# A tile of their own for the score maxima, the row sums finished on VectorE, spread reciprocals a slot later, and early weights converted one step a period

## Chip, cores and metric

The kernel runs on one core of a Trainium2 chip. The metric is the device time of one execution in microseconds (us).

## What is computed

Causal attention over 2 batches, 12 heads, 448 positions and 64 features a head, and then two gated layers over the 896 tokens:

```python
scores = scale * np.matmul(q, k.transpose(0, 1, 3, 2))
scores = np.where(mask, -1000000000.0, scores)
scores = scores - np.max(scores, axis=-1, keepdims=True)
attn = np.exp(scores)
attn = attn / (np.sum(attn, axis=-1, keepdims=True) + 1e-09)
x = np.matmul(attn, v)                            # regrouped to 896 x 768
x = (1/(1+exp(-(x @ w_gate))) * (x @ w_val)) @ moe_w_out
h = x @ w_in                                      # 896 x 1024
solu = h * softmax(h); ln = normalised solu * g_ln
out = ln @ moe2_w_out                             # 896 x 768
```

## The kernel before

All five engines run instruction streams in an order that is written out by hand (`manual_schedule`). Each engine takes its own stream in order, so an instruction that waits holds up everything behind it on its engine. Waits between engines follow from which tiles, and which parts of them, instructions read and write. Matrix products are made exact enough by splitting each operand into a rounded hi part and a lo remainder and multiplying three pairs of parts.

**The attention stage** handles 12 head pairs (`NPR`), one every 8 slots (`PER`, a period). The table `STEPS` gives each step a slot relative to the start of its pair, an engine and a function; the loop over slots `s` emits for each slot the TensorE steps first ('E'), then ScalarE ('A'), VectorE ('D') and GpSimd ('P'). A pair's steps reach over some 23 slots, so three pairs overlap. For one pair p, with the slots before the change:

- keys and queries: casts on GpSimd (`prep_k_hi`, slot -7, and `prep_q_hi`, -6) and remainders on VectorE (`prep_k_lo`, -5, line 229, and `prep_q_lo`, -2, line 249). `prep_q_lo(p)` also issues the load of pair p+2 on SP's queue. Pair 0 is prepared ahead of the loop.
- scores: `sc_mm` at slots 0 and 4 puts the causal mask into PSUM with bf16 matmuls (line 329) and adds the score matmuls (line 338). Query tiles 3 and 0 (448 and 64 keys) share one PSUM tile, tiles 2 and 1 (320 and 192 keys) another.
- `sc_max` on VectorE (slots 0, 1, 4, 5; line 351, for the very first tile line 349) writes negated row maxima; `sc_exp` on ScalarE (slots 1, 2, 5, 6; line 358) makes the exponentials and the row sums. Maxima and sums of a pair lie in one tile of 16 columns, `sum_t`: sums in columns 0 to 7, maxima in 8 to 15, those of one query tile four columns apart (`8 + i:16:NQ`).
- `sums` on GpSimd (slot 7, line 363) adds an epsilon to the sums, `recips` on VectorE (slot 8, line 367) takes reciprocals, `rs_wide` on GpSimd spreads them over columns (slot 8, line 221), `rs_mm` on TensorE transposes them (slot 10, line 381) and `rs_out` on ScalarE copies the result out of PSUM (slot 11).
- the exponentials are transposed on TensorE (`tr_mm`, slots 9, 11, 13, 15; line 409), cast on ScalarE a slot later (`tr_hi`, line 416) and their remainder taken on VectorE two slots later (`tr_lo`, line 229); two PSUM tiles take turns. The products with the values are eight chunks on TensorE (`pv_mm`, slots 13 to 20; line 441).
- the values are split on GpSimd (`prep_v_hi`, slot 7, and `prep_v_lo`, 9); `last_keys` is a small GpSimd copy (3). `x_mul` on VectorE multiplies by the reciprocals (21), `x_hi` on ScalarE casts (22) and `x_lo` on GpSimd takes the remainder (23).

`keep_warm(n)` issues n small matmuls whose result nobody reads (line 308): 56 ahead of the loop and 24 each at slots 2, 5 and 9.

**Weights** arrive as 64-bit floats, 768 KB a chunk, and are converted in four steps (`bits_steps`): a scaling on ScalarE (line 112), then a shift (115) and two combinations (117, 120) on VectorE; after the last step the next chunk's load is issued on SP's queue. `chunk_hi` (ScalarE, 131) and `chunk_lo` (VectorE, 134) split a chunk. In the attention stage the loop converts chunks 0 to 3, one every nine slots from slot 88 on, and splits chunks 0 and 1.

**The early tile.** From slot 96 on (`PER * NPR`) the loop emits up to two matmuls a slot of the next stage's first tile (`early_tiles`, line 473; 36 in all, 18 with each of chunks 0 and 1), as far as their chunk has been split. What is left follows the loop. The next stage then starts at line 574; its `start_chunk(c)` splits chunk c+1 and converts chunk c+2 if nobody has.

Of the kernel before, what the change touches and what calls it, by code (L numbers as in the profile page):

```python
# [44 lines left out]
def attn_moe_moe2(ctx: ExitStack, tc: tile.TileContext, qk, v, w_gv, w_out, w_in2, w_out2, g_ln, out):  # L45
# [16 lines left out]
    maskb = const.tile([128, 128], BF16, name="maskb")  # L62
# [127 lines left out]
    with ExitStack() as actx:  # L190
# [94 lines left out]
        nc.vector.tensor_copy(out=maskb, in_=mask0)  # L285
# [6 lines left out]
        sum_t = [one.tile([128, 16], F32, name=f"sum{i}") for i in range(3)]  # L292
# [26 lines left out]
        def sc_mm(p, g):  # L319
            both = ps_s.tile([128, 2, 512], F32, tag="s", name="s")  # L320
            t = qk_sp[p]
            flat = t.rearrange("p c s -> p (c s)")
            c0 = 0
            for i in GROUPS[g]:
                n = QE[i]
                w = min(n, 128)
                ps = ps_sc[p, i] = both[:, :, c0:c0 + n]
                for e in range(2):
                    nc.tensor.matmul(out=ps[:, e, n - w:], lhsT=identb, rhs=maskb[:, 128 - w:],
                                     start=(c0 == 0), stop=False, skip_group_check=True)  # L330
                c0 += n
            for i in GROUPS[g]:
                n = QE[i]
                for m, (cq, ck) in enumerate(((1, 0), (1, 3), (2, 0))):

                    for e in range(2):
                        rows = slice(e * D, (e + 1) * D)
                        nc.tensor.matmul(out=ps_sc[p, i][:, 1 - e], lhsT=flat[rows, cq * S + n - 128:cq * S + n],  # L338
                                         rhs=t[rows, ck, :n], start=False, stop=(m == 2), skip_group_check=True)

        def sums_of(p, i, e):
            k = NQ * (1 - e) + i
            return sum_t[p % 3][:, k:k + 1], sum_t[p % 3][:, 8 + k:9 + k]

        def sc_max(p, i):
            ps = ps_sc[p, i]
            if p == 0 and i == GROUPS[0][0]:
                for e in range(2):
                    nc.vector.reduce_max(out=sums_of(p, i, e)[1], in_=ps[:, 1 - e], axis=AX.X, negate=True)
            else:  # L350
                nc.vector.reduce_max(out=sum_t[p % 3][:, 8 + i:16:NQ], in_=ps, axis=AX.X, negate=True)  # L351
# [9 lines left out]
        def sums(p):  # L361
            rs = rs_t[p] = st.tile([128, 16], F32, tag="rs", name="rs")
            nc.gpsimd.tensor_scalar(out=rs[:, 8:16], in0=sum_t[p % 3][:, 0:8], scalar1=EPS_SUM, scalar2=0.0,
                                    op0=ALU.add, op1=ALU.add)

        def recips(p):
            nc.vector.reciprocal(out=rs_t[p][:, 0:8], in_=rs_t[p][:, 8:16])
# [93 lines left out]
        def early_tiles():  # L461
# [30 lines left out]
            (10, 'E', rs_mm),  # L492
            (-7, ENG['kh'], prep_k_hi), (-6, ENG['qh'], prep_q_hi), (-5, ENG['kl'], prep_k_lo), (-2, 'D', prep_q_lo),
            (3, ENG['lk'], last_keys), (7, ENG['vh'], prep_v_hi), (9, ENG['vl'], prep_v_lo),
            (7, 'P', sums), (8, 'D', recips), (8, ENG['rx'], rs_wide), (11, ENG['rr'], rs_out),
# [6 lines left out]

        def steps(s, eng):
            for s0, e, f in STEPS:
                p, r = divmod(s - s0, PER)
                if e == eng and r == 0 and (1 if s0 < 0 else 0) <= p < NPR:
                    f(p)


        for s in range(PER * NPR + 26):  # L510
            if s in (2, 5, 9):
                keep_warm(24)
# [4 lines left out]
            steps(s, 'A')  # L517
            steps(s, 'D')
            steps(s, 'P')
            if s in (8, 12):  # L520
                dma_next()

            for c in range(2 * NE + 2):
                e = s - 88 - 9 * c
                if e == 0:
                    bits_now = bits_steps(c)
                if e in (0, 2, 4, 6):
                    next(bits_now)
                if e == 7 and c < 2 * NE:
                    chunk_hi(c)  # L530
                if e == 8 and c < 2 * NE:
                    chunk_lo(c)
# [230 lines left out]
```

## Time and profile before

| what | us |
|---|---|
| median of 3 runs | 514.14 |
| lowest and highest of them | 513.76, 514.71 |
| the profiled execution, its own time | 514.3 |
| its span, first to last instruction | 512.5 |
| TensorE busy (98% of the span) | 501.2 |
| VectorE busy (66%) | 335.9 |
| ScalarE busy (44%) | 226.4 |
| GpSimd busy (23%) | 118.0 |

In the profile PE is TensorE, PEld its weight loads, DVE VectorE, ACT ScalarE, POOL GpSimd and SP the engine that issues the DMAs. L351 is line 351 of the kernel. A row of the timeline gives start, duration, engine, line, operation, output tile and input tiles, shapes and count; square brackets hold the idle time of the engine before it and what ended that. Times are from the start of the span. Busy time of TensorE is partly modelled, and an average over stages with different limits.

### The profile page before, as it was taken

What the parts mean: (1) busy time and instruction counts of PE and PEld (TensorE: products, weight loads), DVE (VectorE), ACT (ScalarE), POOL (GpSimd) and SP (SyncE); (2) the same over time, 40 slices, a digit from 0 to 9 for tenths busy, and PEclk for the clock granted to TensorE, in tenths of its full rate; (3) what the DMA queues carried; (4) which work ended last, traced back from release to release, by engine and by line L of the source; (5) the groups of instructions that cost most, each with busy time, mean ns of one, the idle gap of its engine ahead of it and who ended that gap; (6) DMA issues with size and microseconds to landing.
All of it is one profiled execution on the core that took longest, in us unless ns stands there. A gap on an engine that the chain in (4) does not pass through costs nothing.

```text
span 512.5 us, 7699 instructions
## 1 busy us (share of the span) xinstructions
PE 501.2 (98%) x2980; PEld 457.1 (89%) x2980; DVE 335.9 (66%) x512; ACT 226.4 (44%) x481; POOL 118.0 (23%) x203
## 2 busy tenths in 40 slices
PE   8899999989999999999999999999999999999997
PEld 8888888878899999999999999999998888899997
DVE  4578787887655777887777766766753887841210
ACT  4677777784532454345434432343324242432211
POOL 3375757552000000000000000000050587710000
PEclk9899999999999999999999999999999999999999
DMA  5632323112333154355433532354440221000101
GB/s 150 184 92 77 92 79 93 42 49 76 125 123 99 66 165 164 125 163 161 137 116 125 182 123 68 139 165 164 133 176 1 86 100 62 0 32 33 61 32 61
DMA packets 13204, 52.79 MB, mean 103 GB/s; under 512 B 1776, under 2 KB 2288, under 8 KB 13168
## 3 DMA queue, kind: packets, MB, share of 16 engines
q1 hardware_dynamic: 13168, 52.31, 31.4%
q8 instruction: 23, 0.38, 0.3%
q14 instruction: 13, 0.11, 0.1%
HBM read 49.55 MB, written 2.75 MB: 102 GB/s over the span
## 4 chain that ended last, share of the span: by engine, by line
PE 81%; DVE 6%; ACT 6%; POOL 5%; issue 1%; POOLq 0%; ACTq 0%
PE gv L574 33%; PE pm L604 17%; PE po L695 12%; PE h L634 11%; ACT p L358 4%; DVE sum L351 4%; POOL v L229 2%; DVE qks L229 2%; PE gv L473 1%; PE warm L308 1%; POOL rx L221 1%; PE tp L677 1%; PE x L441 1%; PE s L338 1%; PE t L409 1%
## 5 line engine op out<-in xcount | busy, mean ns | idle before, releaser
L574 PE MATMUL gv<-xy,hl 128*128 128x448 f32 x828 | 168.1, 365 | 0.6 <-ACT pre L478 0.6
L574 PEld LDWEIGHTS gv<-xy,hl 128*128 128x128 f32 x828 | 155.5, 188 | 13.2 <-ACT pre L478 1.0
L604 PE MATMUL pm<-g,hl 128*128 128x448 f32 x432 | 87.7, 365 | 0.0
L604 PEld LDWEIGHTS pm<-g,hl 128*128 128x128 f32 x432 | 81.2, 188 | 6.4
L621 POOL TENSOR_SCALAR t<-t,g_sb 128x768 f32<-128x768 f32 x8 | 9.0, 1123 | 248.1 <-PE pm L604 248.1
L134 DVE TENSOR_TENSOR hl<-t,hl 128x768 fp32r<-128x768 f32 x36 | 35.1, 975 | 40.2 <-ACT hl L131 38.4
L695 PE MATMUL po<-wo,lt 128*128 128x384 f32 x336 | 60.7, 340 | 0.0
L634 PE MATMUL h<-wi,xy 128*128 128x512 f32 x252 | 59.2, 395 | 0.0
L695 PEld LDWEIGHTS po<-wo,lt 128*128 128x128 f32 x336 | 58.7, 188 | 0.2 <-POOL wo L626 0.2
L358 ACT ACTIVATE p<-s,sum 128x448 f32<-128x448 f32 (+3 forms) x96 | 45.0, 478 | 29.9 <-DVE sum L351 14.9
L634 PEld LDWEIGHTS h<-wi,xy 128*128 128x128 f32 x252 | 47.2, 188 | 11.4
L120 DVE SCALAR_TENSOR_TENSOR t<-raw,t 128x768 int32<-128x768 int32 (+1 forms) x56 | 53.0, 946 | 1.7
L117 DVE SCALAR_TENSOR_TENSOR t<-raw,t 128x768 int32<-128x768 int32 (+1 forms) x56 | 52.6, 939 | 1.8
L441 PE MATMUL x<-pt,v 128*128 128x320 f32 (+3 forms) x252 | 53.5, 327 | 0.0
L112 ACT ACTIVATE raw<-raw 128x768 f32<-128x768 f32 (+1 forms) x56 | 47.9, 866 | 10.3 <-DMA raw<-in_wo_dram 6.0
L351 DVE TENSOR_REDUCE sum<-s 128x2 f32<-128x128 f32 (+3 forms) x47 | 31.6, 672 | 15.2 <-ACT p L358 13.4
L441 PEld LDWEIGHTS x<-pt,v 128*128 128x128 f32 x252 | 38.1, 190 | 2.0
L229 DVE TENSOR_TENSOR pt<-t,pt 128x512 fp32r<-128x512 f32 (+1 forms) x48 | 31.9, 667 | 3.8 <-ACT pt L416 3.8
L115 DVE TENSOR_SCALAR t<-raw 128x768 int32<-128x768 int32 (+1 forms) x56 | 30.6, 547 | 4.9 <-ACT raw L112 4.9
L171 DVE TENSOR_TENSOR lt<-tp,lt 128x512 fp32r<-128x512 f32 x14 | 9.7, 690 | 36.4 <-ACT lt L170 36.4
L131 ACT CAST hl<-t 128x768 fp32r<-128x768 f32 x36 | 30.0, 832 | 4.6 <-PE pm L604 4.2
L179 ACT ACTIVATE wk<-gv 128x448 f32<-128x448 f32 x23 | 11.3, 542 | 43.1 <-PE gv L574 43.1
(90 smaller groups left out, 542.7 us busy)
## 6 DMA issues: line engine op xcount, KB each, us to landing
raw<-in_gv_dram SPq DMA_DIRECT2D x24, 768.0 KB, 4.4
raw<-in_wo_dram SPq DMA_DIRECT2D x20, 768.0 KB, 4.3
raw<-in_wi_dram SPq DMA_DIRECT2D x12, 512.0 KB, 3.5
qkr<-in_qk_dram SPq DMA_DIRECT2D x22, 224.0 KB, 3.5
vr<-in_v_dram SPq DMA_DIRECT2D x12, 256.0 KB, 2.6
out_dram<-o SPq DMA_DIRECT2D x6, 384.0 KB, 2.3
qkr<-in_qk_dram SPq DMA_DIRECT2D x4, 112.0 KB, 2.7
out_dram<-o SPq DMA_DIRECT2D x2, 192.0 KB, 1.8
```

The source lines that it names most:

```text
L112: nc.scalar.activation(out=w1.bitcast(F32), in_=w1.bitcast(F32), func=AF.Copy, scale=2.0 ** -112)
L117: nc.vector.scalar_tensor_tensor(out=tt, in0=w1, scalar=-2 ** 31, in1=tt, op0=ALU.bitwise_and, op1=ALU.bitwise_or)
L120: nc.vector.scalar_tensor_tensor(out=tt, in0=w0, scalar=29, in1=tt, op0=ALU.logical_shift_right, op1=ALU.bitwise_or)
L134: nc.vector.tensor_tensor(out=lo, in0=t_t.pop(it), in1=f32(hi), op=ALU.subtract)
L229: (nc.gpsimd if eng == 'P' else nc.vector).tensor_tensor(out=out, in0=a, in1=b, op=ALU.subtract)
L351: nc.vector.reduce_max(out=sum_t[p % 3][:, 8 + i:16:NQ], in_=ps, axis=AX.X, negate=True)
L358: nc.scalar.activation(out=p_t[(2 * p + e) % NPB][:, POFF[i]:POFF[i] + n], in_=ps[:, 1 - e], func=AF.Exp, bias=mx, scale=1.0, accum_out=sm)
L441: nc.tensor.matmul(out=ps[:, 128 * j:], lhsT=l, rhs=pt_t[h][:, c, u, c0:c0 + S - 128 * j], start=(chunk == 0 and n == 0), stop=(chunk == 7 ...
L574: nc.tensor.matmul(out=ps[i, b], lhsT=w[:, a, cs], rhs=xy[kk][:, x, b * S:(b + 1) * S], start=(kk == 0 and a == 0 and x == 0), stop=(kk == ...
L604: nc.tensor.matmul(out=ps[b], lhsT=w[:, a, cs], rhs=g_t[kk][:, x, b * S:(b + 1) * S], start=(kk == 0 and a == 0 and x == 0), stop=(kk == N ...
L634: nc.tensor.matmul(out=h[:, n * 512:(n + 1) * 512], lhsT=xy[kk][:, a, tk], rhs=wi[n * NK + kk][:, c], start=(kk == 0 and i == 0), stop=(kk ...
L695: nc.tensor.matmul(out=ps[n], lhsT=lts[k // 4][:, a, k % 4], rhs=wo[k][:, c, cs], start=(k == 0 and i == 0), stop=(k == NF2 - 1 and i == 2))
```

## The change

- The maxima get a tile of their own, `max_t`, with the two maxima of a query tile side by side; `sum_t` keeps the eight sums.
- `sums` on GpSimd is gone; `recips` (slot 8) adds the epsilon and takes the reciprocals, both on VectorE.
- `rs_mm` moves from slot 10 to 11, `rs_out` from 11 to 12.
- The mask tile is 64 columns wider (a second copy on VectorE at the start), so that query tiles 3 and 0 get their masks with two matmuls instead of four.
- The preparation of pair 1 no longer follows the table: its GpSimd casts are emitted at slot 0, its VectorE remainders (and with them the load of pair 3) at slot 1, ahead of slot 1's maxima.
- `keep_warm` at slot 9 has 12 matmuls, not 24.
- Chunks 0 and 1 are converted one step a period: the steps of chunk 0 stand at slots 18, 26, 34 and 42, its `chunk_hi` at 43 and `chunk_lo` at 46; those of chunk 1 at 50, 58, 66, 74, 75 and 78. Each is emitted behind everything else in its slot. Chunk 2 is converted at slots 114 to 117; chunk 3 no longer in this loop, so `start_chunk(1)` does it.

```diff
--- before.py
+++ after.py
@@ -59,7 +59,7 @@
     ident = const.tile([128, 128], F32, name="ident")
     identx = const.tile([128, 128], F32, name="identx")
     identb = const.tile([128, 128], BF16, name="identb")
-    maskb = const.tile([128, 128], BF16, name="maskb")
+    maskb = const.tile([128, 192], BF16, name="maskb")
     g_sb = const.tile([128, NF2], F32, name="g_sb")
     mhalf = const.tile([128, 1], F32, name="mhalf")
 
@@ -282,14 +282,17 @@
         nc.gpsimd.tensor_copy(out=identx[:, D:], in_=ident[:, :D])
         nc.gpsimd.affine_select(out=mask0, in_=mask0, pattern=[[-1, 128]], compare_op=ALU.is_ge,
                                 fill=NEG, base=0, channel_multiplier=1)
-        nc.vector.tensor_copy(out=maskb, in_=mask0)
+        nc.vector.tensor_copy(out=maskb[:, :128], in_=mask0)
+        nc.vector.tensor_copy(out=maskb[:, 128:], in_=mask0[:, 64:])
         zero = one.tile([128, 3 * D], F32, name="zero")
         nc.vector.memset(zero, 0.0)
 
         v2 = [one.tile([128, 2, 3, 3 * D], FR, name=f"v2_{i}") for i in range(2)]
 
         v3 = [one.tile([128, 2, 2 * D], FR, name=f"v3_{i}") for i in range(2)]
-        sum_t = [one.tile([128, 16], F32, name=f"sum{i}") for i in range(3)]
+
+        sum_t = [one.tile([128, 8], F32, name=f"sum{i}") for i in range(3)]
+        max_t = [one.tile([128, NQ, 2], F32, name=f"max{i}") for i in range(3)]
         NPB = 4
         p_t = [one.tile([128, POFF[NQ]], F32, name=f"p{i}") for i in range(NPB)]
 
@@ -322,13 +325,13 @@
             flat = t.rearrange("p c s -> p (c s)")
             c0 = 0
             for i in GROUPS[g]:
-                n = QE[i]
-                w = min(n, 128)
-                ps = ps_sc[p, i] = both[:, :, c0:c0 + n]
+                ps_sc[p, i] = both[:, :, c0:c0 + QE[i]]
+                c0 += QE[i]
+
+            for n, (lo, hi) in enumerate(((320, 512),) if g == 0 else ((192, 320), (384, 512))):
                 for e in range(2):
-                    nc.tensor.matmul(out=ps[:, e, n - w:], lhsT=identb, rhs=maskb[:, 128 - w:],
-                                     start=(c0 == 0), stop=False, skip_group_check=True)
-                c0 += n
+                    nc.tensor.matmul(out=both[:, e, lo:hi], lhsT=identb, rhs=maskb[:, :hi - lo],
+                                     start=(n == 0), stop=False, skip_group_check=True)
             for i in GROUPS[g]:
                 n = QE[i]
                 for m, (cq, ck) in enumerate(((1, 0), (1, 3), (2, 0))):
@@ -340,7 +343,7 @@
 
         def sums_of(p, i, e):
             k = NQ * (1 - e) + i
-            return sum_t[p % 3][:, k:k + 1], sum_t[p % 3][:, 8 + k:9 + k]
+            return sum_t[p % 3][:, k:k + 1], max_t[p % 3][:, i, 1 - e:2 - e]
 
         def sc_max(p, i):
             ps = ps_sc[p, i]
@@ -348,7 +351,7 @@
                 for e in range(2):
                     nc.vector.reduce_max(out=sums_of(p, i, e)[1], in_=ps[:, 1 - e], axis=AX.X, negate=True)
             else:
-                nc.vector.reduce_max(out=sum_t[p % 3][:, 8 + i:16:NQ], in_=ps, axis=AX.X, negate=True)
+                nc.vector.reduce_max(out=max_t[p % 3][:, i], in_=ps, axis=AX.X, negate=True)
 
         def sc_exp(p, i):
             n = QE[i]
@@ -358,13 +361,10 @@
                 nc.scalar.activation(out=p_t[(2 * p + e) % NPB][:, POFF[i]:POFF[i] + n], in_=ps[:, 1 - e], func=AF.Exp,
                                      bias=mx, scale=1.0, accum_out=sm)
 
-        def sums(p):
+        def recips(p):
             rs = rs_t[p] = st.tile([128, 16], F32, tag="rs", name="rs")
-            nc.gpsimd.tensor_scalar(out=rs[:, 8:16], in0=sum_t[p % 3][:, 0:8], scalar1=EPS_SUM, scalar2=0.0,
-                                    op0=ALU.add, op1=ALU.add)
-
-        def recips(p):
-            nc.vector.reciprocal(out=rs_t[p][:, 0:8], in_=rs_t[p][:, 8:16])
+            nc.vector.tensor_scalar(out=rs[:, 8:16], in0=sum_t[p % 3], scalar1=EPS_SUM, scalar2=None, op0=ALU.add)
+            nc.vector.reciprocal(out=rs[:, 0:8], in_=rs[:, 8:16])
 
 
 
@@ -489,10 +489,10 @@
               for u, a, s0 in ((1, 0, 9), (1, 1, 11), (0, 0, 13), (0, 1, 15))
               for d, eng, f in ((0, 'E', tr_mm), (1, 'A', tr_hi), (2, 'D', tr_lo))),
             *((13 + n, 'E', lambda p, n=n: pv_mm(p, n)) for n in range(len(CHUNKS))),
-            (10, 'E', rs_mm),
+            (11, 'E', rs_mm),
             (-7, ENG['kh'], prep_k_hi), (-6, ENG['qh'], prep_q_hi), (-5, ENG['kl'], prep_k_lo), (-2, 'D', prep_q_lo),
             (3, ENG['lk'], last_keys), (7, ENG['vh'], prep_v_hi), (9, ENG['vl'], prep_v_lo),
-            (7, 'P', sums), (8, 'D', recips), (8, ENG['rx'], rs_wide), (11, ENG['rr'], rs_out),
+            (8, 'D', recips), (8, ENG['rx'], rs_wide), (12, ENG['rr'], rs_out),
             (21, 'D', x_mul), (22, ENG['xh'], x_hi), (23, ENG['xl'], x_lo),
             (1, 'A', lambda p: sc_exp(p, 3)), (2, 'A', lambda p: sc_exp(p, 0)),
             (5, 'A', lambda p: sc_exp(p, 2)), (6, 'A', lambda p: sc_exp(p, 1)),
@@ -500,36 +500,45 @@
             (4, 'D', lambda p: sc_max(p, 2)), (5, 'D', lambda p: sc_max(p, 1)),
         )
 
+
+        weights = {}
+        for c in range(2 * NE):
+            it = bits_steps(c)
+            for k in range(4):
+                weights[PER * (2 + 4 * c + k) + 2] = lambda it=it: next(it)
+            weights[PER * (2 + 4 * c + 3) + 3] = lambda c=c: chunk_hi(c)
+            weights[PER * (2 + 4 * c + 3) + 6] = lambda c=c: chunk_lo(c)
+        two = bits_steps(2 * NE)
+        for k in range(4):
+            weights[PER * NPR + 18 + k] = lambda: next(two)
+
         def steps(s, eng):
             for s0, e, f in STEPS:
                 p, r = divmod(s - s0, PER)
-                if e == eng and r == 0 and (1 if s0 < 0 else 0) <= p < NPR:
+                if e == eng and r == 0 and (2 if s0 < 0 else 0) <= p < NPR:
                     f(p)
 
 
         for s in range(PER * NPR + 26):
             if s in (2, 5, 9):
-                keep_warm(24)
+                keep_warm(24 if s < 9 else 12)
             steps(s, 'E')
             for _ in range(2):
                 if s >= PER * NPR and left and next(early):
                     left -= 1
             steps(s, 'A')
+            if s == 1:
+                prep_k_lo(1)
+                prep_q_lo(1)
             steps(s, 'D')
             steps(s, 'P')
+            if s == 0:
+                prep_k_hi(1)
+                prep_q_hi(1)
             if s in (8, 12):
                 dma_next()
-
-            for c in range(2 * NE + 2):
-                e = s - 88 - 9 * c
-                if e == 0:
-                    bits_now = bits_steps(c)
-                if e in (0, 2, 4, 6):
-                    next(bits_now)
-                if e == 7 and c < 2 * NE:
-                    chunk_hi(c)
-                if e == 8 and c < 2 * NE:
-                    chunk_lo(c)
+            if s in weights:
+                weights[s]()
         while left:
             left -= next(early)
         for t in range(NE):
```

## Rows read from the trace of the kernel before

**Rows 1.** chain of waits, attention period and after: start us, us, what

```profile
66.68 0.47 ACT xy L219
67.14 0.83 ACT p L358 x4
...
129.50 168.07 PE gv L574 x828
```

**Rows 2.** timeline, VectorE, 59 to 69 us (columns as explained above)

```profile
62.22 0.29 DVE L351 TENSOR_REDUCE sum<-s 128x2 f32<-128x128 f32 x1 [0.87 <-ACT p L358]
62.70 0.69 DVE L229 TENSOR_TENSOR pt<-t,pt 128x512 fp32r<-128x512 f32 x1 [0.18 <-ACT pt L416]
63.30 0.98 DVE L229 TENSOR_TENSOR qks<-qkr,qks 128x448 fp32r<-128x448 f32 x1
...
66.76 0.62 DVE L249 SCALAR_TENSOR_TENSOR qks<-qkr,qks 128x448 fp32r<-128x448 f32 x1
...
68.33 0.20 DVE L367 RECIPROCAL rs<-rs 128x8 f32<-128x8 f32 x1 [0.42 <-POOL rs L363]
68.45 1.04 DVE L351 TENSOR_REDUCE sum<-s 128x2 f32<-128x896 f32 x1
```

**Rows 3.** timeline, ScalarE, first wide exponentials of pairs 1, 2, 3 and 11

```profile
16.41 0.63 ACT L358 ACTIVATE p<-s,sum 128x448 f32<-128x448 f32 x1 [1.57 <-DVE sum L351]
...
26.20 0.63 ACT L358 ACTIVATE p<-s,sum 128x448 f32<-128x448 f32 x1 [1.17 <-DVE sum L351]
...
34.68 0.63 ACT L358 ACTIVATE p<-s,sum 128x448 f32<-128x448 f32 x1 [1.15 <-POOL xy L229]
...
104.48 0.64 ACT L358 ACTIVATE p<-s,sum 128x448 f32<-128x448 f32 x1 [0.33 <-POOL xy L229]
```

**Rows 4.** timeline, TensorE's weight loads, 59 to 69 us

```profile
61.42 0.14 PEld L381 LDWEIGHTS r<-identx,rx 128*128 128x128 f32 x1 [0.53 <-POOL rx L221]
...
66.90 0.23 PEld L329 LDWEIGHTS <-identb 128*128 128x128 bf16 x4
```

**Rows 5.** waits of VectorE, 0 to 20 us: us in total, times, longest us

```profile
DVE sum L351 <- ACT p L358: 4.1, 3, 1.5
```

**Rows 6.** timeline, TensorE, 12 to 17 us

```profile
14.47 0.72 PE L338 MATMUL s<-qks 64*128 64x448 f32 x8 [1.74 <-DVE qks L249]
```

**Rows 7.** windows: length, busy PE, PEld, DVE, ACT, POOL, granted clock, DMA, GB/s

```profile
16.00:17.00 1.00, 1.00 (x12) 1.00 (x11) 0.37 (x1) 0.59 (x2) 1.00 (x3) 0.50 0.85 272
```

**Rows 8.** timeline, GpSimd, 59 to 69 us

```profile
61.86 1.42 POOL L229 TENSOR_TENSOR v<-vr,v 128x384 fp32r<-128x384 f32 x2
63.24 0.57 POOL L234 TENSOR_SCALAR qks<-qkr 128x448 fp32r<-128x448 f32 x1
```

**Rows 9.** timeline, VectorE, 23 to 36 us: key remainder of pair 3

```profile
28.66 0.62 DVE L229 TENSOR_TENSOR qks<-qkr,qks 128x448 fp32r<-128x448 f32 x1
```

**Rows 10.** page, costliest groups: busy us, mean ns of one, idle before

```profile
L117 DVE SCALAR_TENSOR_TENSOR t<-raw,t 128x768 int32<-128x768 int32 (+1 forms) x56 | 52.6, 939 | 1.8
...
L112 ACT ACTIVATE raw<-raw 128x768 f32<-128x768 f32 (+1 forms) x56 | 47.9, 866 | 10.3 <-DMA raw<-in_wo_dram 6.0
...
L115 DVE TENSOR_SCALAR t<-raw 128x768 int32<-128x768 int32 (+1 forms) x56 | 30.6, 547 | 4.9 <-ACT raw L112 4.9
```

**Rows 11.** timeline, ScalarE, 59 to 69 us

```profile
65.12 0.53 ACT L358 ACTIVATE p<-s,sum 128x320 f32<-128x320 f32 x1 [0.95 <-DVE sum L351]
```

**Rows 12.** timeline, all engines, 113 to 130 us

```profile
119.97 1.14 POOL L229 TENSOR_TENSOR xy<-xf,xy 128x448 fp32r<-128x448 f32 x1 [3.27 <-ACT xy L219]
120.00 1.93 DVE L120 SCALAR_TENSOR_TENSOR t<-raw,t 128x768 int32<-128x768 int32 x1
```

**Rows 13.** timeline, TensorE, 110 to 116 us

```profile
110.34 0.30 PE L409 MATMUL t<-identx,p 128*128 128x128 f32 x1 [0.58 <-DVE pt L229]
...
112.74 0.30 PE L409 MATMUL t<-identx,p 128*128 128x128 f32 x1 [0.90 <-DVE rs L367]
...
115.05 0.33 PE L381 MATMUL r<-identx,rx 128*128 128x128 f32 x1 [0.55 <-POOL rx L221]
```

## The prediction

> **What bounds the kernel now.** I read the page first: TensorE is busy for nearly all of the span, which suggests that only less work on TensorE can help. Then I read the chain of waits, and in the attention stage it names other engines: from one head pair to the next the path runs through ScalarE, GpSimd and VectorE [rows 1]. Its last exponentials (67.14 and 0.83) end at 67.97, the GpSimd addition of the sums follows, then the reciprocals and the next 448-wide maxima on VectorE at 68.45 [rows 1, 2]. That is a closed loop: maxima, exponentials, cast, subtraction, key remainder, maxima, exponentials, sums. A pair takes 8.725 us: the first wide exponentials of pairs 3 and 11 start at 34.68 and 104.48, 69.80 us for eight periods [rows 3]. TensorE's weight loads stand idle 0.53 us in each period, for the spread reciprocals [rows 4]; this is the loop showing through, since TensorE issues without another long gap. From 129.50 on the chain is one block of TensorE work [rows 1]; the change does not reach it, except that one conversion moves there.
>
> **Sum.** The profiled execution took 514.3 us, of which the span is 512.5; I add to 514.3 and take off 0.16 at the end, since the median is 514.14.
>
> **Start-up.** VectorE loses 4.1 us in three waits of a maximum for exponentials that belong to other columns of the same tile [rows 5]. With a tile of their own these maxima need not wait. The first of the three waits is refilled by the key and query remainders of pair 1, two instructions of about 0.61 us; they moved ahead, so the score matmuls of pair 1 lose their 1.74 us wait [rows 6]. On the loop I count one such wait, 1.2 (4.1 less twice the longest, 1.5, leaves 1.1 at the least), and 0.14 for the shorter step to the next maxima, worked out below: 1.3 us. Pair 1 then took 9.79 us (16.41 to 26.20 [rows 3]) because TensorE came late: behind that wait, behind 24 warming matmuls, and at a granted clock of 0.50, which is 1.2 GHz [rows 7]. Now 12 warming matmuls stand there. Without the lateness pair 1 would take about 7.9: the 8.36 of the next part less the cast of x, 0.47 [rows 1], which that pair does not have. That is 1.9 more, together 3.2. I take **-3.0**; the bounds are -1.3 (TensorE stays late) and -3.4. The earlier GpSimd casts of pair 1 stay where their input lands; the earlier load of pair 3 has a period more to land. The second mask copy on VectorE falls in its wait for the first keys; uncovered, it costs no more than a 64-wide maximum, 0.3.
>
> **The steady period.** First, the sums. Now 0.48 us pass from the last exponential to the maxima. After: a short VectorE addition, bounded by the reciprocals (0.20 [rows 2]), then the reciprocals, whose successor starts 0.12 after them: 0.02 + 0.20 + 0.12 = 0.34. Saved 0.14. Second, the maxima's tile: VectorE waits 0.87 before the 64-wide maxima, but the instruction behind them needs a ScalarE cast and starts at 62.70, after another 0.18 of waiting [rows 2]. So this wait goes and the wait for the cast takes its place: nothing on the loop, but a hole of about 1.1 us in VectorE's queue. Third, GpSimd: its queue was held by the sums, ahead of x's remainder. Without them that remainder and all that follows starts about 0.8 us earlier, so the scaled-query cast at 63.24 [rows 8] will be over before the key remainder at 63.30, which took 0.98 beside it [rows 2] and 0.62 where nothing stood beside it [rows 9]. That period, 26.20 to 34.68, was 8.48. So the new period is 8.48 - 0.14, and 0.02 more for score matmuls that then end last: 8.36. Nine periods lie between the exponentials of pairs 2 and 11: 0.12 for the first, 8 x 0.365 for the others, **-3.1**; bounds 0 and -4. The reciprocals' transposes a slot later remove the 0.53, but the transposes then first in line wait for VectorE's subtraction at nearly the same moment: late next, nothing gained by itself. Two mask matmuls fewer shorten a 0.23 us group of four weight loads [rows 4] by some 0.1; TensorE has slack, so nothing, and 0.1 in the last period.
>
> **Conversions into the periods.** Eight steps and two pairs of hi and lo move from slots 88 to 105 to slots 18 to 78, one period each. Alone they take 0.87 on ScalarE and 0.55, 0.94 and 0.94 on VectorE [rows 10]; lo, with two inputs of the same size, I put at 0.95. A ScalarE step must fit in a hole of 0.95 [rows 11] that shrinks by the 0.3 the maxima come earlier: 0.2 each, 0.4. The hi cast, of similar length, 0.1 each, 0.2. The VectorE steps stand in the 1.1 us hole, but GpSimd's value remainder (1.42 us, two instructions [rows 8]) runs there, and two-input VectorE work waits for such an instruction: one step took 1.93 beside a GpSimd subtraction that started with it and took 1.14 [rows 12]. Behind the first instruction the step ends 0.1 to 0.2 late and pushes GpSimd's query cast back onto the key remainder, up to 0.36: 0.4 each for four long steps, 1.6; 0.1 for the two short ones, 0.2. The lo subtraction stands in slot 6 behind the query remainder (66.76 [rows 2]) with no hole: 0.95 less 0.1 of drain and 0.15 of idle before the sums, 0.7; if x's remainder gets in first, 1.14 [rows 12] more. X's remainder becomes ready with the end of x's cast, at 67.14 [rows 1], the lo with the end of the query remainder, 66.76 and some 0.55: too close to tell, so I take 1.4 each, 2.8. Sum **+5.2**; bounds 2 and 8. Each last step issues the next weight load on SP, 768 KB, a period or more before it is due and ahead of that period's query load; hidden, or some tenths if not.
>
> The Trainium skill, SBUF — State Buffer, section Who interferes with whom, says that the port pair of VectorE and GpSimd is an exclusive lock: whoever starts first holds it for a whole instruction and the other fully blocks. By that rule each meeting costs all that is left of the other instruction, which the 1.93 of [rows 12] agrees with and the 0.98 of [rows 2] with less; with full blocks the conversions come to some 6.9, an estimate from the same rows (1.84 for each lo, 0.6 for each long step), and the time to 512.8. The lock case below is the rule at its worst.
>
> **The tail.** With both chunks ready at slot 96 the 36 early matmuls start there, and the conversions leave VectorE. TensorE's waits of 0.58, 0.90 and 0.55 [rows 13] go, with 0.1 of masks: **-2.1**; from there TensorE issues closely, so no more is to be had. Bounds -1 and -3. The fourth chunk's conversion moves behind the stage's end, 3.3 us on VectorE and ScalarE beside matmuls that are not due for it for some 10 us: nothing; uncovered, at most those 3.3.
>
> Sum: -3.0 - 3.1 + 5.2 - 2.1 = -3.0, 511.3; less 0.16, **511.1 us**.
>
> **Rivals.** *Conversions nearly free* (0.25): lo gets in before x's remainder and the steps fit the hole; they cost 2, the time is 507.9. For it: lo and x's remainder become ready within 0.2 us of each other; against: GpSimd is busy in the hole. *The period does not shorten* (0.15): the waits only change names, because the key remainder still meets a GpSimd cast once the steps push it back; the -3.1 goes and the time is 514.2. For it: the wait at 62.70 follows right behind the one removed. *Lock, slower* (0.08): each VectorE step waits for both value instructions, 1.42, and then pushes the loop: (1.42 + 0.95 - 1.1) x 4 = 5.1, short steps 0.9 x 2, key remainder 0.36 x 6, lo 1.85 x 2, ScalarE 0.6, in all 13.4, and 519.3. It decides from 8.2 on, the sum of the gains. Against it: 1.42 is two instructions with a gap. *Clock* (0.07): with 12 warming matmuls TensorE stays at half rate beyond the start-up; each us at it costs about half a us, 3 to 6 us of it bring 512.6 to 514.1.
>
> **Numbers.** A measurement of this kernel can tell about 0.2%, 1.03 us. The forecast has 0.45, its own range being 509 to 513, all of it faster by more than that. Faster: 0.45 + 0.25, 0.05 of the unshortened period and 0.02 of the clock, 0.77. Same: 0.10 and 0.02, 0.12. Slower: the lock and 0.03 of the rest, 0.11. The range, 507.0 to 514.2, takes in the free conversions and the unshortened period and leaves out the lock case and the edges of the others.
>
> **What would show it.** Right: no maxima waiting for exponentials; in periods without conversions, wide exponentials about 8.36 apart and key remainders of 0.62; periods with a lo 1.5 to 2 longer; the first pair-2 exponentials near 23; no TensorE wait for the reciprocals. Wrong: periods still 8.7, lo subtractions of about 1 us beside an idle GpSimd, conversions above 2 us, a granted clock under 1 after 20 us, or a TensorE wait for weights at the third or fourth chunk.

## The result, and the profile after

The changed kernel takes 521.58 us (median of 4 runs, 520.81 to 521.82) against 513.95 of the kernel before (513.73 to 514.71). The ratio is 1.0143 [1.0126, 1.0161]: 1.4% slower, outside the range of the prediction and on its other side. The profiled execution took 521.75 us with a span of 519.9, against 514.3 and 512.5.

The stretches between a few starts that both timelines show, in us:

| stretch | before | after | difference |
|---|---|---|---|
| span's start to the first wide exponentials | 9.20 | 10.10 | +0.9 |
| from there to those of pair 2 | 17.00 | 14.67 | -2.3 |
| pair 2 to pair 11, nine periods | 78.27 | 85.31 | +7.0 |
| pair 11 to the next stage's first matmul (line 574, now 583) | 25.03 | 22.20 | -2.8 |
| gate, value and w_out matmuls (lines 574 and 604, now 583 and 613) | 255.63 | 260.65 | +5.0 |
| the rest | 127.37 | 126.97 | -0.4 |

The starts of the nine periods come from ScalarE's timeline after, which answers to [rows 3]; the first row is pair 2, the last two are pairs 10 and 11:

```profile
24.78 0.63 ACT L361 ACTIVATE p<-s,max 128x448 f32<-128x448 f32 x1 [1.17 <-DVE max L354]
33.72 0.63 ACT L361 ACTIVATE p<-s,max 128x448 f32<-128x448 f32 x1 [1.27 <-DVE max L354]
42.75 0.63 ACT L361 ACTIVATE p<-s,max 128x448 f32<-128x448 f32 x1 [1.28 <-DVE max L354]
52.17 0.63 ACT L361 ACTIVATE p<-s,max 128x448 f32<-128x448 f32 x1 [1.28 <-DVE max L354]
63.01 0.63 ACT L361 ACTIVATE p<-s,max 128x448 f32<-128x448 f32 x1 [2.68 <-DVE max L354]
...
101.18 0.63 ACT L361 ACTIVATE p<-s,max 128x448 f32<-128x448 f32 x1 [2.67 <-DVE max L354]
110.08 0.63 ACT L361 ACTIVATE p<-s,max 128x448 f32<-128x448 f32 x1 [1.28 <-DVE max L354]
```

The periods are 8.95, 9.03, 9.42, 10.83, and then 8.89, 9.03, 9.43, 10.82, 8.90; before they were 8.71 to 8.74 after a first one of 8.48. The long ones hold the last step of a chunk, its hi and its lo. The shortest is still longer than before.

VectorE's timeline after, one period without a conversion, answers to [rows 2]:

```profile
101.01 0.68 DVE L229 TENSOR_TENSOR pt<-t,pt 128x512 fp32r<-128x512 f32 x1
102.56 0.29 DVE L354 TENSOR_REDUCE max<-s 128x2 f32<-128x128 f32 x1 [0.87 <-ACT p L361]
103.03 0.69 DVE L229 TENSOR_TENSOR pt<-t,pt 128x512 fp32r<-128x512 f32 x1 [0.18 <-ACT pt L416]
103.64 0.61 DVE L229 TENSOR_TENSOR qks<-qkr,qks 128x448 fp32r<-128x448 f32 x1
104.63 0.82 DVE L354 TENSOR_REDUCE max<-s 128x2 f32<-128x640 f32 x1 [0.38 <-PE s L341]
...
108.36 0.44 DVE L366 TENSOR_SCALAR rs<-sum 128x8 f32<-128x8 f32 x1
108.83 0.20 DVE L367 RECIPROCAL rs<-rs 128x8 f32<-128x8 f32 x1
108.95 1.04 DVE L354 TENSOR_REDUCE max<-s 128x2 f32<-128x896 f32 x1
```

GpSimd's timeline, same stretch:

```profile
107.59 1.18 POOL L229 TENSOR_TENSOR xy<-xf,xy 128x448 fp32r<-128x448 f32 x1 [2.08 <-ACT xy L219]
```

Three things are to be seen. The 64-wide maxima wait 0.87 for the wide exponentials, to the digit as before, though sums and maxima lie in two tiles. The key remainder takes 0.61, not 0.98, and the 0.37 come back as a wait of the next maxima for TensorE's scores, 0.38. The new addition takes 0.44 and ends at 108.80, as x's remainder ends on GpSimd (107.59 and 1.18 make 108.77).

The two blocks of the gate, value and w_out matmuls are in the chain of waits after, which answers to [rows 1]:

```profile
59.27 1.83 DVE hl L134
...
97.46 1.83 DVE hl L134
...
132.28 171.37 PE gv L583 x828
303.66 89.28 PE pm L613 x432
```

Both lo subtractions stand in the chain. The 828 matmuls took 168.07 before [rows 1]; the 432 took 87.56, so a matmul takes 206.7 ns from start to start where it took 202.7, on the same tiles, with no waits in the block and at a granted clock of 1.00. No term of the prediction concerned this.

The half clock of [rows 7] is not in every execution of the kernel before (the clock over a whole execution is 0.997 or less in 56 of 97 executions of it and of the experiments that keep its start, in none of 59 with the changed start), and executions with it take some 0.8 us longer.

### The profile page after: what moved, and what is told of

Read it like the earlier page. It is cut to its first block, busy times and chain, and to the rows that moved or that the text cites. A ratio compares the mean times of both kernels' runs of the same rounds, so it can differ in the third digit from the quotient of the medians.

```text
span 519.9 us, 7598 instructions
## 1 busy us (share of the span) xinstructions
PE 505.2 (97%) x2944; PEld 454.7 (87%) x2944; DVE 338.1 (65%) x525; ACT 225.9 (43%) x481; POOL 115.7 (22%) x191
## 4 chain that ended last, share of the span: by engine, by line
PE 81%; DVE 9%; ACT 7%; issue 2%; POOL 0%; ACTq 0%; POOLq 0%
PE gv L583 33%; PE pm L613 17%; PE h L643 11%; PE po L704 11%; ACT p L361 5%; DVE max L354 4%; DVE pt L229 2%; PE gv L473 2%; PE x L441 2%; PE tp L686 1%; PE t L409 1%; PE warm L311 1%; PE s L341 1%; ACT pt L416 1%; DVE qks L229 1%
## 5 line engine op out<-in xcount | busy, mean ns | idle before, releaser
L583 PE MATMUL gv<-xy,hl 128*128 128x448 f32 x828 | 171.4, 368 | 0.6 <-ACT pre L478 0.6
L613 PE MATMUL pm<-g,hl 128*128 128x448 f32 x432 | 89.4, 368 | 0.0
L134 DVE TENSOR_TENSOR hl<-t,hl 128x768 fp32r<-128x768 f32 x36 | 36.4, 1012 | 40.5 <-ACT hl L131 38.7
L361 ACT ACTIVATE p<-s,max 128x448 f32<-128x448 f32 (+3 forms) x96 | 45.0, 478 | 33.0 <-DVE max L354 26.6
L354 DVE TENSOR_REDUCE max<-s 128x2 f32<-128x128 f32 (+3 forms) x47 | 31.4, 670 | 14.8 <-ACT p L361 12.3
```

Source lines behind the costliest of these rows:

```text
L134: nc.vector.tensor_tensor(out=lo, in0=t_t.pop(it), in1=f32(hi), op=ALU.subtract)
L354: nc.vector.reduce_max(out=max_t[p % 3][:, i], in_=ps, axis=AX.X, negate=True)
L361: nc.scalar.activation(out=p_t[(2 * p + e) % NPB][:, POFF[i]:POFF[i] + n], in_=ps[:, 1 - e], func=AF.Exp, bias=mx, scale=1.0, accum_out=sm)
L583: nc.tensor.matmul(out=ps[i, b], lhsT=w[:, a, cs], rhs=xy[kk][:, x, b * S:(b + 1) * S], start=(kk == 0 and a == 0 and x == 0), stop=(kk == ...
L613: nc.tensor.matmul(out=ps[b], lhsT=w[:, a, cs], rhs=g_t[kk][:, x, b * S:(b + 1) * S], start=(kk == 0 and a == 0 and x == 0), stop=(kk == N ...
```

## The experiments

On the attention stage the theory was that the conversions cost what the long periods show, that the row of sums costs more on VectorE than on GpSimd, and that the maxima's tile changes nothing, since the scores' PSUM tile still ties maxima and exponentials. On the rhythm of 206.7 ns there were two: **placement**, where tiles lie in SBUF (the changed mask tile is 128 bytes larger a partition), and **entry**, how TensorE's work stands when it comes into the stage.

**e1_shift**, the kernel before with a larger mask tile:

```diff
-    maskb = const.tile([128, 128], BF16, name="maskb")
+    maskb = const.tile([128, 192], BF16, name="maskb")
...
```

> The kernel before with one edit: the mask tile is declared 64 columns wider and the new columns are never used, so all SBUF tiles behind it lie 128 bytes further. Placement theory: the matmuls of the gate and value stage and of the next one start every 206.7 ns instead of 202.7 as in the changed kernel, which is 5.0 us over 1260 matmuls; attention stays as before; about 519 us. Rival, that the slower matmuls come from the changed order of the work or from the shorter TensorE program: no change, 514 us, 202.7 ns.

Measured: 513.95 us, ratio 0.9997 [0.9988, 1.0007]; the 828 matmuls take 168.07, as before: nothing here for placement. Its profiled execution has no half clock: pair 0 to pair 2 is 15.36 instead of 17.00. So 1.65 of the 2.3 gained there is that episode of half clock.

**e2_pad256**, the changed kernel with the mask tile 256 wide:

```diff
-    maskb = const.tile([128, 192], BF16, name="maskb")
+    maskb = const.tile([128, 256], BF16, name="maskb")
...
```

> The changed kernel with its mask tile widened by 64 more columns, so that the tiles behind it lie 256 bytes further than before instead of 128. Placement theory with a period of 256 bytes: matmuls of 448 columns go back to 202.7 ns, 516.6 us. Placement with a longer period, or the rival that the order of the work slows them: 206.7 ns and 521.6 us as in the changed kernel.

Measured: 521.86 us, 1.0145 [1.0127, 1.0163]; 171.37 us for the 828. So placement by 128 or 256 bytes is not the cause. What such a shift does is small and cancels: the 512-column matmuls of h go from 234.2 to 233.3 ns and the 384-column ones of the output from 175.8 to 177.5.

**e3_oldconv**, the changed kernel with the old conversions (the loop over `c` with `e = s - 88 - 9 * c` in place of `weights`):

```diff
...
-            if s in weights:
-                weights[s]()
+            for c in range(2 * NE + 2):
+                e = s - 88 - 9 * c
...
```

> The changed kernel with the weight conversions put back to slots 88 and later, all else as changed. If the conversions in the periods cost 5.2 us there and give back 2 to 3 at the end of the stage: wide exponentials 8.90 us apart throughout, no period of 10.8, and 2 to 3 us faster than the changed kernel, about 519. If they are free there (the rival): the same 521.6 or slower, since the end of the stage gets longer.

Measured: 513.12 us, 0.9982 [0.9972, 0.9992]. Periods are 8.89, all but the first (8.95); the 828 matmuls take 168.07. The tail is 24.40. From its nine periods (80.08) to the changed kernel's (85.31) are 5.2, the conversions' price, and from those before (78.27) 1.8, the price of the rest. So the conversions cost what the long periods show, and the slow rhythm comes with their new slots too; the forecast of about 519 had left the rhythm slow. Up to the gate and value stage this trace and that of the changed kernel hold 1040 matmuls each, that of the kernel before 1076. So the shorter program alone, the rival named with e1_shift, does not make the rhythm slow.

**e4_oldsums**, the changed kernel with the sums on GpSimd:

```diff
...
-            nc.vector.tensor_scalar(out=rs[:, 8:16], in0=sum_t[p % 3], scalar1=EPS_SUM, scalar2=None, op0=ALU.add)
+            nc.gpsimd.tensor_scalar(out=rs[:, 8:16], in0=sum_t[p % 3], scalar1=EPS_SUM, scalar2=0.0,
...
-            (8, 'D', recips), (8, ENG['rx'], rs_wide), (12, ENG['rr'], rs_out),
+            (7, 'P', sums), (8, 'D', recips), (8, ENG['rx'], rs_wide), (12, ENG['rr'], rs_out),
```

> The changed kernel with the addition to the sums back on GpSimd at slot 7, all else as changed. If the addition on VectorE waits for the GpSimd remainder of x that now runs ahead of it (0.44 us instead of about 0.2): with it back, the step from the last exponentials to the wide maxima goes from 0.63 to about 0.48, periods without conversions from 8.90 to about 8.75, and the kernel is about 1.4 us faster. Rival, that the addition is hidden and the period is set by TensorE alone: periods stay at 8.90.

Measured: 518.88 us, 1.0091 [1.0073, 1.0108]. Periods without work are 8.76, those with a lo 9.77. Besides the addition, the lo has changed. The timeline of all engines around it, changed kernel:

```profile
59.12 1.17 POOL L229 TENSOR_TENSOR xy<-xf,xy 128x448 fp32r<-128x448 f32 x1 [2.61 <-ACT xy L219]
59.19 1.92 DVE L134 TENSOR_TENSOR hl<-t,hl 128x768 fp32r<-128x768 f32 x1
```

and this kernel, in the same period:

```profile
59.41 0.95 DVE L134 TENSOR_TENSOR hl<-t,hl 128x768 fp32r<-128x768 f32 x1
...
60.15 0.32 POOL L366 TENSOR_SCALAR rs<-sum 128x8 f32<-128x8 f32 x1 [2.72 <-ACT p L361]
...
60.55 1.14 POOL L229 TENSOR_TENSOR xy<-xf,xy 128x448 fp32r<-128x448 f32 x1
```

With the sums ahead of it, x's remainder starts behind the lo, which then takes 0.95 instead of 1.92. So the row costs more on VectorE, and twice: 0.13 for the addition in a period without work (8.89 to 8.76; 0.02 to 0.04 in one with a step), and about 1 for each lo. That second part is why the gain is 2.7 us and not the 1.4 that was expected. By the Trainium skill, SBUF — State Buffer, section Who interferes with whom, the later of two that need the shared port pair waits for the whole of the other's instruction; the trace agrees to 0.13 (60.29, where x's remainder ends, and 0.95 make 61.24, the lo ended at 61.11).

**e7_maxtile**, the kernel before with only the maxima's tile:

```diff
...
-        sum_t = [one.tile([128, 16], F32, name=f"sum{i}") for i in range(3)]
+        sum_t = [one.tile([128, 8], F32, name=f"sum{i}") for i in range(3)]
+        max_t = [one.tile([128, NQ, 2], F32, name=f"max{i}") for i in range(3)]
...
```

> The kernel before with the maxima in a tile of their own and nothing else. If the 64-wide maxima wait for the wide exponentials because both read the same PSUM bank, and not because of the shared columns: the wait of 0.87 stays in every period, periods stay at 8.73, time 513.8. Rival, the prediction's reason: the wait goes, and the 0.18 wait for the cast grows to 1.05.

Measured: 513.80 us, 1.0001 [0.9991, 1.0010]; periods 8.71 to 8.74. The waits of VectorE, 30 to 100 us (total, times, longest), are those of the kernel before, which also has 7.0, 8 and 0.9:

```profile
DVE max L352 <- ACT p L359: 7.0, 8, 0.9
```

The tile changes nothing. What the two instructions still share is the PSUM tile in which query tiles 3 and 0 lie, and `max_t`, out of which the exponentials read other columns. That other columns of one tile make no such wait is seen in the kernel before, at its start (VectorE and ScalarE):

```profile
10.57 0.29 DVE L351 TENSOR_REDUCE sum<-s 128x2 f32<-128x128 f32 x1 [1.47 <-ACT p L358]
...
11.21 0.31 ACT L358 ACTIVATE p<-s,sum 128x64 f32<-128x64 f32 x1
...
11.31 0.82 DVE L351 TENSOR_REDUCE sum<-s 128x2 f32<-128x640 f32 x1
...
13.33 0.56 DVE L351 TENSOR_REDUCE sum<-s 128x2 f32<-128x384 f32 x1 [1.19 <-ACT p L358]
```

The maxima of query tile 2 (11.31) start while the exponentials of tile 0 run (11.21 and 0.31), although both use `sum_t`; their scores lie in two PSUM tiles. The maxima of tiles 0 and 1 (10.57, 13.33) wait for exponentials whose scores lie in the same PSUM tile as theirs. So the PSUM tile is the cause that is left, by these waits and by exclusion. By the Trainium skill, PSUM — Partial Sum Buffer, section PSUM bank collisions raise a hardware error, two engines must not touch one bank on the same partitions at once, reads included, so a program has to order them; the 0.87 agrees. No run gave the 64-wide maxima a PSUM tile of their own.

**e8_front**, the changed kernel with the VectorE steps of pairs 3 to 5 and 7 to 9 emitted ahead of the 64-wide maxima, where VectorE waits, instead of behind:

```diff
+            if i == 0 and p in (3, 4, 5, 7, 8, 9):
+                weights.pop(PER * p + 2)()
```

> The changed kernel with the six VectorE conversion steps moved ahead of the 64-wide maxima of their period, where VectorE waits 0.87 for ScalarE, instead of behind them. If the steps cost their time because there is no hole behind the maxima: the periods with a long step go from 9.42 to about 9.0, those with both a long step and a lo from 10.83 to about 10.4, and the kernel gains about 1.7 us. Rival, that what costs is the meeting with GpSimd in the port: no gain, 521.6.

Measured: 518.69 us, 1.0096 [1.0079, 1.0114]; periods 8.89, and 10.43 with a lo. The longest step, on VectorE:

```profile
50.85 1.55 DVE L120 SCALAR_TENSOR_TENSOR t<-raw,t 128x768 int32<-128x768 int32 x1
52.32 0.28 DVE L356 TENSOR_REDUCE max<-s 128x2 f32<-128x128 f32 x1
```

A step in the hole ahead of the maxima is free even at 1.55 us; behind them it cost 0.14 (9.03 less 8.89), 0.53 (9.42) or, for the last one, 0.4 (10.83 to 10.43). A lo costs 1.54 (10.43 less 8.89). Only the order was changed, so this shows where the hole in VectorE's queue is: still ahead of the maxima.

**e6_norow**, the kernel before with the reciprocals straight from the sums and their transposes two slots later. The 1e-9 that is added to a sum is left out (a sum is at least 1):

```diff
...
-            (10, 'E', rs_mm),
+            (12, 'E', rs_mm),
...
-            (7, 'P', sums), (8, 'D', recips), (8, ENG['rx'], rs_wide), (11, ENG['rr'], rs_out),
+            (8, 'D', recips), (8, ENG['rx'], rs_wide), (13, ENG['rr'], rs_out),
```

> The kernel before, its conversions and all else, but the reciprocals are taken straight from the sums (the addition of 1e-9 is left out, and with it the GpSimd instruction), and the transposes of the reciprocals stand at slot 12, behind the score matmuls, their copy at slot 13. If a period is bound by the loop of VectorE and ScalarE, and by the TensorE stretch from the subtraction of slot 1 to the second scores: the step from the exponentials to the maxima shrinks from 0.48 to 0.15, the reciprocals' 0.4 leave that stretch, and periods go from 8.73 to about 8.1 to 8.3, the kernel to 509 or 510. Rival, that TensorE's whole work bounds the period: 8.7 and 513.8.

Measured: 517.69 us, 1.0070 [1.0055, 1.0085]; periods 9.17. A miss, with its cause on ScalarE:

```profile
66.98 0.53 ACT L219 COPY rb<-r 128x448 f32<-128x448 f32 x1 [1.25 <-PE r L377]
67.41 0.53 ACT L358 ACTIVATE p<-s,sum 128x320 f32<-128x320 f32 x1
```

The copy of the spread reciprocals waits 1.25 us for TensorE with the exponentials behind it. Two slots are too late, so this run tells nothing of the row.

**e5_nudge**, the changed kernel with one idle matmul into a fresh PSUM tile ahead of the gate and value stage. The stage's first matmul overwrites it:

```diff
                     ps[i, b] = psg.tile([128, S], F32, tag="gv", name="gv")
+                    if c == 0:
+                        nc.tensor.matmul(out=ps[i, b][:, :128], lhsT=identb, rhs=identb, start=True, stop=True)
```

> The changed kernel with one idle 128x128 bf16 matmul ahead of the first accumulation of the gate and value stage; its result is overwritten. Phase theory: the 206.7 ns between the matmuls there is a steady pattern into which weight loads and matmuls fall at the stage's start, so one instruction more at that start can bring the 202.7 ns pattern of the kernel before, some 516.6 us in all. Rival, that something which lasts through the stage slows each matmul: 206.7 ns and 521.6 us as before.

Measured: 516.05 us, 1.0040 [1.0027, 1.0052]. TensorE's timeline at the stage's start:

```profile
132.00 0.22 PE L577 MATMUL gv<-identb 128*128 128x128 bf16 x1 [0.62 <-ACT pre L478]
132.02 2.27 PE L585 MATMUL gv<-xy,hl 128*128 128x448 f32 x10
```

and the chain of waits:

```profile
132.21 167.86 PE gv L585 x828
300.07 87.56 PE pm L615 x432
```

Pair 2 to pair 11 is 85.31 here too. One matmul more makes the interval of 1260 others 4 ns shorter, and the median falls from 521.58 by 5.5 us. So nothing that lasts through the stage makes the rhythm slow; how TensorE enters it decides. In the single records of the traces the first interval between the stage's matmuls is 315 ns in all six kernels with the slow rhythm, 308 or 309 in the five with the fast one and no idle matmul, and 286 in the three with it. What makes it so is not shown.

**e9_holes**, the changed kernel with the sums on GpSimd as in e4_oldsums, the steps ahead of the maxima as in e8_front, and each lo there too, a period later:

```diff
...
+            for k in range(1, 4):
+                front[2 + 4 * c + k] = lambda it=it: next(it)
...
-            weights[PER * (2 + 4 * c + 3) + 6] = lambda c=c: chunk_lo(c)
+            front[2 + 4 * c + 4] = lambda c=c: chunk_lo(c)
...
```

> The changed kernel with three repairs: the addition to the sums back on GpSimd, the VectorE conversion steps ahead of the 64-wide maxima, and each lo there too, one period after its hi. If the periods lose time to the addition waiting in the port, to steps behind the maxima and to lo behind the query remainder: all periods about 8.75, wide exponentials of pairs 2 and 11 about 79 us apart instead of 85.3, the end of the stage as short as in the changed kernel (22.2); 511 us with 202.7 ns between the later matmuls, 516 with 206.7. Rival, that a conversion costs its time wherever it stands: about 82 us between those exponentials, 514 or 519.

Measured: 514.92 us, 1.0013 [1.0004, 1.0023]. Periods are 8.77, all but the first (8.82), so the conversions are free there; the tail is 22.20. The 828 matmuls take 171.37: with the slow rhythm all three repairs only bring the kernel back to the time before.

**e10_direct**, e9_holes with the reciprocals straight from the sums on VectorE (the 1e-9 left out):

```diff
...
-            (7, 'P', sums), (8, 'D', recips), (8, ENG['rx'], rs_wide), (12, ENG['rr'], rs_out),
+            (8, 'D', recips), (8, ENG['rx'], rs_wide), (12, ENG['rr'], rs_out),
```

> As the run with the three repairs, but the addition of 1e-9 is left out and VectorE takes the reciprocals straight from the sums. The step from the last exponentials to the wide maxima then falls from 0.48 to about 0.15. If the loop of VectorE and ScalarE bounds the period with TensorE's copy of the reciprocals out of the way: periods of about 8.45, 76.5 us between the exponentials of pairs 2 and 11, 508.5 us with 202.7 ns, 513.5 with 206.7. Rival, that TensorE bounds it: 8.75 as in the other run.

Measured: 514.54 us, 1.0002 [0.9994, 1.0011]; periods 8.70 to 8.83, not the 8.45 of a period bound by VectorE and ScalarE. With the row shortened VectorE waits for TensorE (waits, 30 to 100 us):

```profile
DVE max L356 <- PE s L341: 3.6, 11, 0.4
```

So the row was not all that kept the period; the path over TensorE is as long.

**e11_direct_nudge**, e10_direct with the idle matmul of e5_nudge:

> The run without the addition, with one idle matmul more ahead of the gate and value stage. Attention as there. Phase theory: the later matmuls fall into one of two rhythms, 202.7 or 206.7 ns, and this run may show the other one than its twin; 5 us between the two then. Rival, that the rhythm comes from the order of the work before the stage: the same rhythm in both.

Measured: **509.18 us, 0.9902 [0.9888, 0.9917]**, 1.0% faster than before, the fastest here. The chain of e10_direct, then of this one:

```profile
124.83 171.38 PE gv L585 x828
296.21 89.28 PE pm L615 x432
```

```profile
124.53 167.86 PE gv L587 x828
292.39 87.56 PE pm L617 x432
```

The medians are 5.4 us apart, with the same nine periods (78.66). Both leave out the 1e-9; e9_holes, which keeps it, was not run with the idle matmul.

**e12_before_nudge**, the kernel before with the idle matmul:

> The kernel before with one idle matmul more ahead of the gate and value stage, nothing else. Phase theory, where every start of the stage can fall into either rhythm: 202.7 or 206.7 ns, 514 or 519 us. If the idle matmul itself sets the fast rhythm: 202.7 ns, 514 us, as in the changed kernel with it. Neither should change the attention stage.

Measured: 514.05 us, 1.0000 [0.9991, 1.0009]; the 828 take 167.85. A stream that has the fast rhythm keeps it; the matmul itself is not what gains.

## Why the prediction was wrong

**Start-up, -3.0.** Pair 0 to pair 2 gave -2.3 against the profiled execution, but -0.7 against e1_shift, which has no half clock. Most of the 1.9 for pair 1's lateness was that episode, which only some executions have: pair 1 took 8.15 without it, and 8.15 after, against my 7.9. The first two terms (1.2 and 0.14) came to 0.7: 7.20 to 6.52 for the first pair. The waits of [rows 5] did not go with the new tile; the first fell from 1.47 to 0.40, because pair 1's remainders now stand in it. VectorE after, 0 to 20 us:

```profile
DVE max L354 <- ACT p L361: 3.0, 3, 1.4
```

Another 0.9 in the other direction lies ahead of the first exponentials, a stretch that is 8.76 to 10.27 in the profiles with the changed start and 9.20 to 10.03 in those with the old one, so I do not put it down to the change. With the old start it is 9.20 and 9.43 in the two profiles with the half clock and 9.88 to 10.03 in the three without: what the episode costs in the whole, 0.8, is less than the 1.65.

**The steady period, -3.1** (0.12 and 8 x 0.365 make 3.04). It was +1.8: 0.47 in the first period, 8.48 to 8.95, and some 0.17 in each of the eight others. Here the mechanism failed, in three steps.
- "Second, the maxima's tile ... this wait goes": it stayed, as e7_maxtile shows. I took the tile of the sums and maxima for the cause; the runs leave the PSUM tile of the scores, which I did not list. So the "hole of about 1.1 us" behind the maxima was not there; it stayed ahead of them, as 0.87.
- "First, the sums ... saved 0.14": I bounded the addition by the 0.20 of the reciprocals without asking which GpSimd instruction now runs at that moment. The instruction that it used to hold up, x's remainder, does, and the addition takes 0.44. With that the period is 0.13 longer than with the sums on GpSimd (e4_oldsums), not 0.14 shorter.
- The third step came true, the key remainder at 0.61 to 0.65 from the second period on, and was worth nothing. The next maxima need it and TensorE's scores, for which I added 0.02, and the path over TensorE is as long. Before, the step from the end of the subtraction at 60.67 (0.68) to those maxima at 64.26 took 2.91, and the scores ended at 64.22; after, from 101.69 to 104.63, 2.94. My base of 8.48 was the one period in which this step took 2.60, because the reciprocals' transposes had started ahead of the subtraction's end (26.52 against 26.70). Moved a slot, they stand behind the other transposes but still ahead of the scores, in every period; so the first period lost 0.35 by them, and the rest gained nothing. VectorE and TensorE, before:

```profile
26.02 0.68 DVE L229 TENSOR_TENSOR pt<-t,pt 128x512 fp32r<-128x512 f32 x1
26.52 0.27 PE L381 MATMUL r<-identx,rx 128*128 128x128 f32 x1
...
29.30 0.82 DVE L351 TENSOR_REDUCE sum<-s 128x2 f32<-128x640 f32 x1
...
60.67 0.68 DVE L229 TENSOR_TENSOR pt<-t,pt 128x512 fp32r<-128x512 f32 x1
61.42 0.33 PE L381 MATMUL r<-identx,rx 128*128 128x128 f32 x1
...
63.20 1.02 PE L338 MATMUL s<-qks 64*128 64x320 f32 x12
...
64.26 0.83 DVE L351 TENSOR_REDUCE sum<-s 128x2 f32<-128x640 f32 x1
```

and TensorE after:

```profile
101.83 0.30 PE L409 MATMUL t<-identx,p 128*128 128x128 f32 x1 [0.51 <-DVE pt L229]
...
102.82 0.27 PE L381 MATMUL r<-identx,rx 128*128 128x128 f32 x1
...
103.57 1.01 PE L341 MATMUL s<-qks 64*128 64x320 f32 x12
```

**Conversions into the periods, +5.2.** They cost 5.2 (e3_oldconv), but not all by the terms given. ScalarE's steps, for which I had 0.4, are free (8.89 in the period with one). The short steps cost 0.14 each (I had 0.1), the long ones 0.53 and 0.4 (0.4), and a lo with its hi 1.54 (1.5). The steps cost this because they stand behind the maxima; the lo because x's remainder got in first, the case to which I gave 1.14, and by e4_oldsums that in turn is due to the sums' move. Two parts of one change met on the port.

**The tail, -2.1.** It is -2.8, of which e3_oldconv has 0.6 without the conversions' move. The waits of [rows 13] are gone; of the waits from 112 us on, 0.22 and the 0.62 at the stage's start are left:

```profile
126.59 0.68 PE L473 MATMUL gv<-xy,hl 128*128 128x448 f32 x2 [0.22 <-ACT pre L478]
132.28 0.88 PE L583 MATMUL gv<-xy,hl 128*128 128x448 f32 x3 [0.62 <-ACT pre L478]
```

**From 129.50 on.** "The change does not reach it" was wrong by 5.0 us. What was computed there is the same; what changed is how TensorE comes into it. Without this, e5_nudge says, the change would still be slower by 0.4%.

**The sum.** I had -3.0 for the whole, the profiled executions say +7.4. The 10.4 between are 4.9 of the steady period (-3.1 to +1.8), 5.0 of the rhythm, 0.7 and 0.9 of the start, 0 of the conversions, less 0.7 of the tail and 0.4 of the rest. The period alone turns the sign, and so would the rhythm alone.

Of the rivals, the lock case came closest in time with 519.3, and by luck: the conversions were to cost 13.4 in it and cost 5.2. "The period does not shorten" came closest in its mechanism, with the clause that the waits only change names; it stopped at 514.2. No rival had a period that becomes longer without a conversion in it, or a change behind the stage.

## What to carry over

Before counting a wait as gone, list every tile that the two instructions share, the PSUM tile that both read as well as the one that is written. Work put into an in-order queue goes ahead of the instruction that waits, not behind it (e8_front: 0.14 to 0.53 us for a step behind, nothing ahead), and a small instruction that changes engine is priced by what runs on the other side of the port at that moment. Look at the mean interval of long matmul blocks that the change "does not reach", too: a change ahead of them can shift it by 2%.

## What was not expected of the hardware

A long stream of 448-column matmuls, each with its weight load, runs in one of two rhythms, 202.7 or 206.7 ns, at a granted clock of 1.00 in both, and keeps over 1260 matmuls the one in which it begins. By their profiles the rhythm is fast before and in e1_shift, e3_oldconv, e6_norow and e7_maxtile; slow after and in e2_pad256, e4_oldsums, e8_front, e9_holes and e10_direct, all six with the new conversion slots; fast in the three with an idle matmul. No kernel's own runs spread by more than 1.6 us, so a kernel does not change over from run to run. What ahead of the stage starts the slow one is open; placement in SBUF by 128 or 256 bytes is not it, nor the number of TensorE instructions alone. The intervals of other matmuls do follow placement: a shift by 128 bytes gives 234.3 and 175.8 ns (512 and 384 columns) where there were 233.3 and 177.7.

An addition over 8 columns took 0.44 us beside a GpSimd subtraction, and 0.16 where GpSimd stood idle (61.56 us in the changed kernel, in a period with a lo).
